# Second MLP product of nine token blocks as seven half-size products, with activation sums on VectorE

## The chip, the cores and the metric

The kernel runs on one core of a Trainium2 chip. The core has a matrix engine (PE, "TensorE"), three engines for elementwise work (DVE = "VectorE", ACT = "ScalarE", POOL = "GpSimd"), a queue engine that issues transfers (SP), and DMA engines that move data between HBM and on-chip memory. Matmul results go into PSUM, eight banks of 512 fp32 columns on 128 partitions; everything else lives in SBUF. The metric is device time of one execution in microseconds (us), lower is better.

## What is computed

Windowed attention with four sink tokens, then an MLP with the activation h·sigmoid(1.702h) and no biases. Cut to what matters:

```python
scores = q @ k.T / 8                        # 4 batches, 8 heads, 768 tokens, 64 wide
keep = (pos_k < 4) | (0 <= pos_q - pos_k < 128)
x = softmax(where(keep, scores, -1e9)) @ v  # -> 3072 tokens x 512
h = x @ w_in                                # 512 -> 2048
g = h / (1 + exp(-1.702 * h))
out = g @ w_out                             # 2048 -> 512
```

## The kernel before

The 3072 tokens are worked on in twelve blocks (`NK` = 12) of 256 tokens (`TB`), three to a batch. For a block `k` the work is: `load` (q, k, v from HBM, then casts to fp16, mostly on POOL from block 2 on), `turn` (q and k transposed: on PE for blocks 0 to 3, by a transposing DMA from block 4 on), `scores` (matmuls into PSUM, exp on ACT into the `at` tiles, the window mask on DVE), `back` (attention times v on PE, `reciprocal` and the normalising multiplication on DVE, transpose to `xT`, by DMA from block 3 on), `mm1` (first MLP product) and `mm2` (second).

`mm1(k)` has eight slices `s`. A slice is two groups of four matmuls with 256 columns into one PSUM bank (L736), a tanh on ACT (L748) and a scalar_tensor_tensor on DVE (L750) that writes one slice of `gT`, twice the activated value in fp16. `mm2(k)` takes the two halves of 128 tokens one after the other (`j`). Each is 16 accumulating matmuls with 512 columns (L765): the stationary operand is 128x128 of `gT`, the moving one a row slice of `w_out16`. ACT then copies the bank, times 0.5, to `osb` (L784), and SP issues two writes of 64 rows (L795). A block has thus 64 matmuls of 256 columns in L736 and 32 of 512 columns in L765.

The order of instructions on each engine is not the program's. Every piece of work is an `Op` with dependencies, a priority and a guessed duration. `Plan.run` plays these through a list scheduler, which also gives out the PSUM banks: seven when the constant masks hold one, with limits by class ("h" for `mm1`, "o" for `mm2`, "s" for scores and so on). The resulting order is then fixed; on the chip each engine runs its list in that order and waits on semaphores where it must. An operation with several possible engines (`plan.any`) gets the one that the plan finds best.

Buffers are rings, and an operation that overwrites a slot depends on the readers of what stood there (`reuse`, `uses`): `qk32`/`v32` (loaded data, RS = 3 slots), `at` (RA = 6), `gT` (RG = 5), `osb` (RO = 3 tiles of 128 tokens). The transfers of the start are chained by hand: a load or weight transfer waits for an earlier one to land (`gates`). The first weight transfer `w0` waits for one of the four q/k pieces of block 1, `o_first[-2]`.

Of the kernel before, what the change touches and what calls it, by code (L numbers as in the profile page):

```python
# [14 lines left out]
P = 128  # L15
# [45 lines left out]
class Plan:  # L61
# [4 lines left out]
    def op(self, eng, dur, lat, fn, deps=(), prio=0.0, acq=None, rel=(), kind=""):  # L66
        return self.any({eng: (dur, lat)}, lambda _: fn(), deps, prio, acq, rel, kind)
# [135 lines left out]
def kernel(  # L203
# [24 lines left out]
    PAIRED_FROM, RR = 2, 3  # L228
    KT, KX, AHEAD = globals().get('OPT',{}).get('KT',4), 3, globals().get('OPT',{}).get('AHEAD',0)
    RB, KM = 4, globals().get('OPT',{}).get('KM',2)  # L230
    RS, RQ, RV, RA, RX, RG, RTH, RO = 3, 2, 4, 6, 3, 5, 3, 3

    pool = ctx.enter_context(tc.tile_pool(name="sb", bufs=1))
    psp = ctx.enter_context(tc.tile_pool(name="ps", bufs=1, space=bass.MemoryType.PSUM))
# [3 lines left out]
    def ring(name, n, shape, dt):  # L238
        return [pool.tile(list(shape), dt, name=f"{name}{i}") for i in range(n)]
# [11 lines left out]
    vs16 = pool.tile([P, B, NP, 2, E], FP16, name="vs16")  # L251
    ks16 = pool.tile([P, B, NP, 32], FP16, name="ks16")
    vs32 = pool.tile([P, B, E], FP32, name="vs32")
    qk32 = ring("qk32", RS, (P, 2, H, 2, D), FP32)
    v32 = ring("v32", RS, (P, H, 2, D), FP32)
    qk16 = ring("qk16", RQ, (P, 2, 2, H, D), FP16)
    v16 = ring("v16", RV, (P, 2, H, E), FP16)
    at = ring("at", RA, (P, 2, 512), FP16)
# [4 lines left out]
    xT = ring("xT", RX, (P, NP, TB), FP16)  # L263
    th = ring("th", RTH, (P, 512), FP16)
    gT = ring("gT", RG, (P, NF, TB), FP16)
    osb = ring("osb", RO, (P, d_model), FP32)
    bank = [psp.tile([P, 512], FP32, name=f"bank{i}") for i in range(8)]

    plan = Plan(8, {"m": 1, "s": 5, "t": 4, "a": 2, "x": 2, "h": RTH, "o": 2})
    op = plan.op  # L270
    half = bank

    def f32(o, i=0):
        return bank[o.banks[i]]
# [372 lines left out]
    def back(k, p):  # L647

        b, r = divmod(k, R)
        u = NP * k + p  # L650
        base = attend(k, 2 * p)
        h8 = L / 8
        A, As = at[u % RA], ats[k % 3]
        vt, vp = v16[k % RV], v16[(k - 1) % RV]

        def avp():
            return f32(o_a)[:, 0 : 4 * E].rearrange("s (j h e) -> s j h e", j=2, h=2)

        def av():
            for j in range(2):  # L660
                if r:
                    blocks = [[(vp, 1, 0), (vt, 0, P)], [(vt, 0, 2 * P), (vt, 1, 3 * P)]][j]
                else:
                    blocks = [[(vt, 0, 0)], [(vt, 0, P), (vt, 1, 2 * P)]][j]
                for i in range(2):
                    mms = [(As[:, bass.ts(j, P)], vs16[:, b, p, i])] if r else []
                    mms += [(A[:, i, c : c + P], src[:, jj, 2 * p + i]) for src, jj, c in blocks]
                    for n, (a_, v_) in enumerate(mms):
                        nc.tensor.matmul(avp()[:, j, i], a_, v_, start=(n == 0), stop=(n == len(mms) - 1))  # L669
# [17 lines left out]
        o_r = op("DVE", 93, 190, lambda: nc.vector.reciprocal(out=rc, in_=avp()[:, :, :, D]),  # L687
                 [o_a], prio=base - 1.2 * h8, kind="rcp")
        o_n = op("DVE", 340, 430, lambda: nc.vector.tensor_tensor(  # L689
            out=X, in0=avp()[:, :, :, 0:D], in1=rc.to_broadcast((P, 2, 2, D)), op=ALU.mult),  # L690
            [o_r] + ([] if k < KX else o_xT["xb", k]), prio=base - 1.2 * h8, rel=[(o_a, 0)], kind="xn")
# [25 lines left out]


    o_g = {}
    n_o = [0]  # L720

    def mm1(k):
        X = xT[k % RX]
# [30 lines left out]
    def mm2(k):  # L754
        b, r = divmod(k, R)
        g = gT[k % RG]
        for j, c0, c1 in ((0, 0, 512), (1, 0, 512)) if k < NK - 1 else ((0, 0, 512), (1, 0, 384), (1, 384, 512)):
            w = c1 - c0
            last = w < d_model
            holder = []  # L760
            prev = None
            for s in range(NS):
                def f(s=s, j=j, holder=holder, c0=c0, c1=c1, w=w):
                    for Fi in (2 * s, 2 * s + 1):
                        nc.tensor.matmul(  # L765
                            f32(holder[0])[:, 0:w], g[:, Fi, bass.ts(j, P)], w_out16[:, Fi, c0:c1],
                            start=(Fi == 0), stop=(Fi == NF - 1),
                        )
                deps = [o_g[k, s], o_w[4 + s // 2]] + ([prev] if prev else [])
                o = op("PE", 2 * pe_ns(w), pe_ns(w) + w / 2.4 + 166, f, deps,  # L770
                       prio=nominal(k + 1, 4 * j + s / 2) + 3 + c0 / 100 * L, acq=None if s else ("o", 1), kind="mm2")
                uses("gT", k % RG, o)
                holder.append(o)
                prev = o
            if not c0:
                oi = n_o[0] % RO
                n_o[0] += 1
                war = reuse("osb", oi)
            O = osb[oi]
# [12 lines left out]
            for i in range(2):  # L792
                eng = "ACT" if i and k == NK - 1 and j else "SP"
                def f(O=O, i=i, row=row, c0=c0, c1=c1, dma=nc.scalar if eng == "ACT" else nc.sync):
                    dma.dma_start(  # L795
                        out[row : row + P, c0:c1].rearrange("(p i) f -> i p f", i=2)[i], O[64 * i : 64 * i + 64, c0:c1]
                    )
                o_d = op(eng, 590, (420, 4), f, o_c, prio=prio, kind="out")
                uses("osb", oi, o_d)

    for j_ in range(8):
        weights(j_, load_at(f"w{j_}"))
    for k_ in range(NK):
        load(k_)
        turn(k_)
        for ps_ in [(0,), (1,), (2,), (3,)] if k_ < PAIRED_FROM else [(0, 1), (2, 3)]:
            scores(k_, ps_)
        for p_ in range(NP):
            back(k_, p_)
        if k_ >= 1:  # L810
            mm1(k_ - 1)
        if k_ >= 2:
            mm2(k_ - 2)
    mm1(NK - 1)
    mm2(NK - 2)
# [82 lines left out]
```

The softmax here doesn't subtract the row's maximum and nothing guards it: scores larger than these inputs give would overflow.

## Time and profile before

Four runs: median 223.15 us, from 221.97 to 224.37.

| from the profile of one execution | |
|---|---|
| this execution's own time | 224.81 us |
| span of the profile | 223.0 us |
| granted TensorE clock, mean | 0.992 of full speed |
| matmuls of the first product (L736) | 768, 100.1 us busy |
| matmuls of the second product (L765, all forms) | 400, 99.8 us busy |
| tanh on ACT (L748) | 96, 603 ns each |
| ACT copies of the second product, 512 columns (L784) | 23, 604 ns each |
| normalising on DVE (L689, both targets) | 48, 422 ns each |
| idle time of ACT ahead of tanh, for PE | 62.5 us |
| DMA traffic | 36.54 MB |

How to read it. A line such as "L765 PE MATMUL bank<-w_out,gT 128\*128 128x512 f16 x368 | 96.3, 379" is a group of like instructions: source line, engine, operation, what it writes and reads, shape, count, then busy time in us and mean duration in ns. Matmuls overlap in the array, so the duration of one is longer than the distance from one to the next. On DVE and ACT too one instruction's record overlaps the next one's a little. Where this text needs what an engine can carry, it takes start-to-start distances out of the timeline. A timeline line is: start us, length us, engine, source line, operation, what it writes and reads, count; in brackets the idle time before and what ended it.

### The profile page before, as it was taken

How to read it: one execution, taken by the hardware profiler on the slowest of the kernel's cores; microseconds unless marked ns; L12 is line 12 of the kernel's file. 1: busy time of each engine (PE TensorE's matmuls, PEld its weight loads, DVE VectorE, ACT ScalarE, POOL GpSimd, SP SyncE). 2: the span in 40 equal slices, each digit the busy share in tenths (PEclk: the TensorE clock that was granted, in tenths of full speed). 3: DMA queues.
4: the chain of work that ended last, by engine and by line, in shares of the span. 5: the costliest groups of instructions: out<-in, count | busy, mean ns of one | idle time of the engine just before them, and what ended most of it. 6: DMA issues, size and time to landing. Idle time of an engine off the chain costs nothing.

```text
span 223.0 us, 5209 instructions
## 1 busy us (share of the span) xinstructions
PE 215.6 (97%) x2066; PEld 145.1 (65%) x2066; DVE 125.8 (56%) x274; ACT 125.6 (56%) x243; POOL 87.2 (39%) x150
## 2 busy tenths in 40 slices
PE   7977999999999999999999999999999999999993
PEld 2445887577766766766666766766667766766642
DVE  3665686278855755665555655765564665634310
ACT  2667655396746764655575575565476475544330
POOL 3568440846991773901923935706600000000000
PEclk9996999999999999999999999999999999999999
DMA  5999999989949869379579289299352222221223
GB/s 195 331 235 205 207 300 240 321 239 235 206 99 218 240 127 273 95 148 255 146 160 303 60 160 309 51 188 285 73 120 49 47 50 47 50 57 37 50 47 94
DMA packets 65911, 36.54 MB, mean 164 GB/s; under 512 B 27968, under 2 KB 61120, under 8 KB 65888
## 3 DMA queue, kind: packets, MB, share of 16 engines
q1 hardware_dynamic: 60848, 30.19, 54.6%
q0 software_dynamic: 4592, 5.37, 12.7%
q10 hardware_dynamic: 448, 0.66, 1.0%
q8 instruction: 16, 0.26, 0.4%
q14 instruction: 7, 0.06, 0.1%
HBM read 27.56 MB, written 6.29 MB: 152 GB/s over the span
## 4 chain that ended last, share of the span: by engine, by line
PE 89%; DMA 1%; ACT 0%; SPq 0%; DVE 0%; issue 0%
PE bank L736 38%; PE bank L765 36%; PE bank L669 7%; PE bank L604 5%; DMA out_dram<-osb 1%; PE bank L532 1%; PE bank L708 1%; PE bank L584 1%; PE bank L596 0%; ACT osb L784 0%; SPq L795 0%; PE bank L325 0%; DVE osb L786 0%
## 5 line engine op out<-in xcount | busy, mean ns | idle before, releaser
L736 PE MATMUL bank<-xT,w_in 128*128 128x256 f16 x768 | 100.1, 273 | 0.0
L765 PE MATMUL bank<-w_out,gT 128*128 128x512 f16 (+2 forms) x400 | 99.8, 371 | 0.0
L748 ACT ACTIVATE th<-bank 128x512 f16<-128x512 f32 x96 | 57.7, 603 | 63.1 <-PE bank L736 62.5
L750 DVE SCALAR_TENSOR_TENSOR gT<-th,bank 128x512 f16<-128x512 f16 x96 | 65.6, 683 | 48.8 <-ACT th L748 47.8
L736 PEld LDWEIGHTS <-w_in 128*128 128x128 f16 x768 | 73.2, 98 | 24.0 <-issue 1.7
L286 POOL CAST qk<-qk 64x512 f16<-64x512 f32 (+1 forms) x74 | 44.8, 609 | 45.3 <-DMA qk<-in_q_dram 42.2
L629 ACT ACTIVATE at<-bank 128x512 f16<-128x512 f32 (+1 forms) x96 | 48.8, 569 | 11.1 <-PE bank L604 10.8
L765 PEld LDWEIGHTS <-gT 128*128 128x128 f16 x400 | 36.1, 98 | 23.3 <-issue 1.4
L636 DVE TENSOR_TENSOR at<-at,bank 128x1024 f16<-128x1024 f16 (+1 forms) x40 | 25.7, 643 | 22.8 <-ACT at L629 22.8
L286 POOL CAST v<-v 64x512 f16<-64x512 f32 (+1 forms) x43 | 26.2, 610 | 10.9 <-DMA v<-in_v_dram 8.9
L669 PE MATMUL bank<-v,at 128*128 128x65 f16 x352 | 21.8, 196 | 2.2 <-ACT at L629 2.0
L669 PEld LDWEIGHTS <-at 128*128 128x128 f16 x352 | 18.1, 99 | 6.3 <-issue 2.1
L784 ACT ACTIVATE osb<-bank 128x512 f32<-128x512 f32 (+1 forms) x24 | 14.4, 600 | 11.0 <-PE bank L765 11.0
L689 DVE TENSOR_TENSOR xb<-bank,rcp 128x256 f16<-128x256 f32 x36 | 15.2, 422 | 0.7
L669 PE MATMUL bank<-vs,ats 128*128 128x65 f16 x128 | 15.3, 196 | 0.0
L604 PEld LDWEIGHTS <-blkT 64*128 64x128 f16 x256 | 8.1, 95 | 9.3 <-issue 7.8
L669 PEld LDWEIGHTS <-ats 128*128 128x128 f16 x128 | 12.3, 100 | 2.0
L604 PE MATMUL bank<-blkT 64*128 64x256 f16 x192 | 13.6, 246 | 0.0
L687 DVE RECIPROCAL rcp<-bank 128x4 f32<-128x4 f32 x48 | 8.4, 177 | 4.7 <-PE bank L669 3.6
L846 PE MATMUL bank<-zero 128*128 128x512 f16 x19 | 6.4, 503 | 1.2 <-DVE zero L304 1.2
L286 ACT COPY blkT<-bank 128x256 f16<-128x256 f16 (+1 forms) x12 | 5.0, 469 | 4.1 <-PE bank L532 4.1
L604 PE MATMUL bank<-blkT,blkT 64*128 64x128 f16 x64 | 7.3, 224 | 0.0
(43 smaller groups left out, 68.9 us busy)
## 6 DMA issues: line engine op xcount, KB each, us to landing
v<-in_v_dram SPq DMA_DIRECT2D x12, 512.0 KB, 7.1
out_dram<-osb SPq DMA_DIRECT2D x46, 128.0 KB, 2.4
qk<-in_q_dram SPq DMA_DIRECT2D x8, 512.0 KB, 5.2
qk<-in_k_dram SPq DMA_DIRECT2D x8, 512.0 KB, 6.4
w_in<-in_moe_w_in_dram POOLq DMA_DIRECT2D x4, 512.0 KB, 8.5
w_out<-in_moe_w_out_dram POOLq DMA_DIRECT2D x4, 512.0 KB, 11.8
qk<-in_q_dram SPq DMA_DIRECT2D x6, 256.0 KB, 5.0
qk<-in_k_dram SPq DMA_DIRECT2D x4, 256.0 KB, 5.2
```

Source lines behind the costliest of these rows:

```text
L286: {"POOL": nc.gpsimd.tensor_copy, "DVE": nc.vector.tensor_copy, "ACT": nc.scalar.copy}[e](out=out, in_=in_)
L604: nc.tensor.matmul(f32(o_s, 2 * n + i)[:, c : c + w], src[d, j], Q[d].rearrange("d j s -> d (j s)")[:, q0 : q0 + w], start=k >= KM, stop=T ...
L629: nc.scalar.activation(out=A[:, i, 0:W], in_=f32(o_s, 2 * n + i)[:, 0:W], func=AF.Exp, scale=scale)
L636: nc.vector.tensor_tensor(out=A[:, :, 0:W], in0=A[:, :, 0:W], in1=mask(c0, c0 + W).unsqueeze(1).to_broadcast((P, 2, W)), op=ALU.mult,)
L669: nc.tensor.matmul(avp()[:, j, i], a_, v_, start=(n == 0), stop=(n == len(mms) - 1))
L687: o_r = op("DVE", 93, 190, lambda: nc.vector.reciprocal(out=rc, in_=avp()[:, :, :, D]), [o_a], prio=base - 1.2 * h8, kind="rcp")
L689: o_n = op("DVE", 340, 430, lambda: nc.vector.tensor_tensor(out=X, in0=avp()[:, :, :, 0:D], in1=rc.to_broadcast((P, 2, 2, D)), op=ALU.mult ...
L736: nc.tensor.matmul(f32(holder[0])[:, bass.ts(e, TB)], w_in16[:, c, bass.ts(Fi, P)], X[:, c] if k < KX else X2[:, :, c], start=(c == 0), st ...
L748: o_t = op("ACT", 477, 600, lambda first=first: nc.scalar.activation(out=th[first.places[0]], in_=f32(first), func=AF.Tanh, scale=0.851), ...
L750: o_g[k, s] = op("DVE", 590, 700, lambda first=first, s=s: nc.vector.scalar_tensor_tensor(out=g[:, 2 * s : 2 * s + 2].rearrange("p a t -> ...
L765: nc.tensor.matmul(f32(holder[0])[:, 0:w], g[:, Fi, bass.ts(j, P)], w_out16[:, Fi, c0:c1], start=(Fi == 0), stop=(Fi == NF - 1),)
L784: nc.scalar.mul(O[:, c0:c1], f32(holder[0])[:, 0:w], 0.5)
```

## The change

Blocks 2 to 10 replace `mm2` by `mm2_by_seven`; blocks 0, 1 and 11 keep `mm2`. The product of a 256x2048 activation block with the 2048x512 weights is cut in two along tokens, along the contraction (even and odd slices of 128) and along the output columns. The 2x2 by 2x2 block product is then done with seven products in place of eight:

- Of the weights, four combinations are formed once (`forms_of_w`): t1 = b12-b11, t2 = b22-t1, t3 = b22-b12, t4 = b21-t2. That is 16 operations of 128x512. Three of the four live in what was the third load slot (tile `third`), which only block 2's load uses any more.
- Of each block's activations, four combinations are formed (`forms_of_g`): s1 = a21+a22, s2 = s1-a11, s3 = a11-a21 (written over a21 in `gT`), s4 = a12-s2; 16 tensor_tensor operations of 128x256 per block, planned on DVE.
- The products s1·t1, a11·b11, s4·b22, s2·t2, s3·t3, a12·b21, a22·t4 are eight matmuls of 256 columns each. Five go into one bank in three stages. After each stage ACT copies what the bank holds, times 0.5, into `part`, and PE then adds the next stage on top. The other two go into a second bank. DVE ends with two operations that scale a bank and add `part`, and SP issues four writes.

Cut to its core:

```diff
-    RS, RQ, RV, RA, RX, RG, RTH, RO = 3, 2, 4, 6, 3, 5, 3, 3
+    RS, RQ, RV, RA, RX, RG, RTH, RO = 3, 2, 4, 4, 3, globals().get('OPT',{}).get('RG',3), 3, 2
+    KS, LASTS = globals().get('OPT',{}).get('KS',2), globals().get('OPT',{}).get('LASTS',NK-1)
...
+    third = pool.tile([P, 3 * H * 2 * D], FP32, name="third")
+    qk32 = ring("qk32", RS - 1, (P, 2, H, 2, D), FP32)
...
+    gF = ring("gF", 2, (P, NS, 3, P), FP16)
+    part = pool.tile([P, 1024], FP32, name="part")
...
-    osb = ring("osb", RO, (P, d_model), FP32)
+    osb = ring("osb", RO, (P, 2 * d_model), FP32)
-    plan = Plan(8, {"m": 1, "s": 5, "t": 4, "a": 2, "x": 2, "h": RTH, "o": 2})
+    plan = Plan(8, {"m": 1, "s": 5, "t": 4, "a": 2, "x": 2, "h": RTH, "o": OPT_("NO", 3)})
...
-        sl = k % RS
+        sl = k if k < RS else (k - 1) % (RS - 1)
...
-        o_n = op("DVE", 340, 430, lambda: nc.vector.tensor_tensor(
-            out=X, in0=avp()[:, :, :, 0:D], in1=rc.to_broadcast((P, 2, 2, D)), op=ALU.mult),
+            for j in range(2):
+                for i in range(2):
+                    nc.scalar.activation(out=X[:, j, i], in_=avp()[:, j, i, 0:D], func=AF.Copy, scale=rc[:, j, i : i + 1])
+        o_n = plan.any({"DVE": (340, 430), **({"ACT": (430, 550)} if OPT_("XA", 3) <= k else {})}, normal,
...
+    def forms_of_g(k):
...
+            for o_, a, b_, what in ((s1, a21, a22, ALU.add), (s2, s1, a11, ALU.subtract), (a21, a11, a21, ALU.subtract), (s4, a12, s2, ALU.subtract)):
...
+    def mm2_by_seven(k):
...
+        m51 = run(2, lambda s: [(0, F[:, s, 0], wf[0][:, s]), (1, G[:, s, 0], W[:, s, 0, 0])], hr,
+                  lambda S: fg(0, S) + fw(0, S), True, ("o", 1))
+        o_1 = op("ACT", 477, 600, lambda: nc.scalar.mul(Z[:, N : 3 * N], f32(hr[0]), 0.5), [m51] + reuse("part", 0), prio=at(), kind="y")
+        m36 = run(2, lambda s: [(0, F[:, s, 2], W[:, s, 1, 1]), (1, F[:, s, 1], wf[1][:, s])], hr,
+                  lambda S: [o_1] + fg(3, S) + fg(1, S) + fw(1, S), False)
+        o_2 = op("ACT", 263, 390, lambda: nc.scalar.mul(Z[:, 0:N], f32(hr[0])[:, N : 2 * N], 0.5), [m36, o_1], prio=at(), kind="y")
+        m7 = run(4, lambda s: [(1, G[:, s, 1], wf[2][:, s])], hr, lambda S: [o_2] + fg(2, S) + fw(2, S), False)
+        o_3 = op("ACT", 263, 390, lambda: nc.scalar.mul(Z[:, 3 * N : 4 * N], f32(hr[0])[:, N : 2 * N], 0.5), [m7, o_2], prio=at(), kind="y")
+        o_v = op("DVE", 600, 700, lambda: nc.vector.scalar_tensor_tensor(
+            out=O.rearrange("p (n c) -> p n c", n=4)[:, 1::2], in0=f32(hr[0]).rearrange("p (n c) -> p n c", n=2), scalar=0.5,
...
+        m24 = run(2, lambda s: [(0, G[:, s, 2], W[:, s, 1, 0]), (1, G[:, s, 3], wf[3][:, s])], hq, lambda S: fw(3, S), True, ("o", 1))
+        o_u = op("DVE", 600, 700, lambda: nc.vector.scalar_tensor_tensor(
...
-            g = o_first[OPT.get("WG", -2)]
+            g = o_first[OPT.get("WG", -1)]
```

More of the change, by code (lines that the diff above doesn't have):

```diff
@@ L253 @@
     vs32 = pool.tile([P, B, E], FP32, name="vs32")
-    qk32 = ring("qk32", RS, (P, 2, H, 2, D), FP32)
-    v32 = ring("v32", RS, (P, H, 2, D), FP32)
+    third = pool.tile([P, 3 * H * 2 * D], FP32, name="third")
+    qk32 = ring("qk32", RS - 1, (P, 2, H, 2, D), FP32)
+    v32 = ring("v32", RS - 1, (P, H, 2, D), FP32)
+    qk32.append(third[:, 0 : 2 * H * 2 * D].rearrange("p (e h i d) -> p e h i d", e=2, h=H, i=2))
+    v32.append(third[:, 2 * H * 2 * D :].rearrange("p (h i d) -> p h i d", h=H, i=2))
+    wf = [third[:, 1024 * n : 1024 * n + 1024].bitcast(FP16).rearrange("p (s c) -> p s c", s=NS) for n in range(3)]
+    wf += ring("wf", 1, (P, NS, d_model // 2), FP16)
+    gF = ring("gF", 2, (P, NS, 3, P), FP16)
+    part = pool.tile([P, 1024], FP32, name="part")
     qk16 = ring("qk16", RQ, (P, 2, 2, H, D), FP16)
@@ L265 @@
     gT = ring("gT", RG, (P, NF, TB), FP16)
-    osb = ring("osb", RO, (P, d_model), FP32)
+    osb = ring("osb", RO, (P, 2 * d_model), FP32)
     bank = [psp.tile([P, 512], FP32, name=f"bank{i}") for i in range(8)]
-    plan = Plan(8, {"m": 1, "s": 5, "t": 4, "a": 2, "x": 2, "h": RTH, "o": 2})
+    OPT_ = globals().get("OPT", {}).get
+    plan = Plan(8, {"m": 1, "s": 5, "t": 4, "a": 2, "x": 2, "h": RTH, "o": OPT_("NO", 3)})
     op = plan.op
@@ L688, in back, with normal @@
                  [o_a], prio=base - 1.2 * h8, kind="rcp")
-        o_n = op("DVE", 340, 430, lambda: nc.vector.tensor_tensor(
-            out=X, in0=avp()[:, :, :, 0:D], in1=rc.to_broadcast((P, 2, 2, D)), op=ALU.mult),
+        def normal(eng):
+            if eng == "DVE":
+                nc.vector.tensor_tensor(out=X, in0=avp()[:, :, :, 0:D], in1=rc.to_broadcast((P, 2, 2, D)), op=ALU.mult)
+                return
+            for j in range(2):
+                for i in range(2):
+                    nc.scalar.activation(out=X[:, j, i], in_=avp()[:, j, i, 0:D], func=AF.Copy, scale=rc[:, j, i : i + 1])
+        o_n = plan.any({"DVE": (340, 430), **({"ACT": (430, 550)} if OPT_("XA", 3) <= k else {})}, normal,
             [o_r] + ([] if k < KX else o_xT["xb", k]), prio=base - 1.2 * h8, rel=[(o_a, 0)], kind="xn")
@@ L719 @@
     o_g = {}
-    n_o = [0]
     def mm1(k):
@@ L775, in mm2 @@
             if not c0:
[L776 to L779, printed above, removed]
+                war = reuse("osb", (k % RO, j))
+            O = osb[k % RO][:, bass.ts(j, d_model)]
             row = k * TB + j * P
@@ L798, in mm2, with forms_of_w, f @@
                 o_d = op(eng, 590, (420, 4), f, o_c, prio=prio, kind="out")
-                uses("osb", oi, o_d)
+                uses("osb", (k % RO, j), o_d)
+    def forms_of_w():
+        W = w_out16.rearrange("p (s e) (h c) -> p s e h c", e=2, h=2)
+        free = [o for (kk, _, _), o in o_cqk.items() if kk == 2] + [o for p in range(NP) for o in o_cv[2, p]]
+        for j in range(4):
+            x = slice(2 * j, 2 * j + 2)
+            b11, b12, b21, b22 = (W[:, x, e, h] for e in range(2) for h in range(2))
+            t1, t2, t3, t4 = (wf[n][:, x] for n in range(4))
+            for n, (o_, a, b_, what) in enumerate(((t1, b12, b11, ALU.subtract), (t2, b22, t1, ALU.subtract),
+                                                   (t3, b22, b12, ALU.subtract), (t4, b21, t2, ALU.subtract))):
+                def f(eng, o_=o_, a=a, b_=b_, what=what):
+                    (nc.gpsimd if eng == "POOL" else nc.vector).tensor_tensor(out=o_, in0=a, in1=b_, op=what)
+                deps = [o_w[4 + j]] + ([o_wf[j, n - 1]] if n in (1, 3) else [])
+                if n == 3:
+                    deps.append(o_wf[j, 1])
+                o_wf[j, n] = plan.any({"POOL": (1110, 1250), "DVE": (450, 550)}, f, deps + (free if n < 3 else []),
+                                      prio=nominal(KS + 1, OPT_("WFP", -9) + j), kind="wf")
@@ new lines, in forms_of_g, with f @@
+    def forms_of_g(k):
+        g, F = gT[k % RG], gF[k % 2]
+        G = g.rearrange("p (s e) (t q) -> p s (e t) q", e=2, t=2)
+        war = reuse("gF", k % 2)
+        w = OPT_("GW", 2)
+        for s in range(0, NS, w):
+            x = slice(s, s + w)
+            a11, a21, a12, a22 = (G[:, x, n] for n in range(4))
+            s1, s2, s4 = (F[:, x, n] for n in range(3))
+            last = [o_g[k, i] for i in range(s, s + w)] + war
+            four = []
+            for o_, a, b_, what in ((s1, a21, a22, ALU.add), (s2, s1, a11, ALU.subtract), (a21, a11, a21, ALU.subtract), (s4, a12, s2, ALU.subtract)):
+                def f(eng, o_=o_, a=a, b_=b_, what=what):
+                    (nc.gpsimd if eng == "POOL" else nc.vector).tensor_tensor(out=o_, in0=a, in1=b_, op=what)
+                o = plan.any({e: {"POOL": (280 * w, 280 * w + 120), "DVE": (OPT_("GD", 105) * w + 60, OPT_("GD", 105) * w + 170)}[e] for e in OPT_("GE", "DVE").split()},
+                             f, last, prio=nominal(k, s + OPT_("GF", 5)) + 3, kind="gf")
+                last = [o]
+                four.append(o)
+            for i in range(s, s + w):
+                o_f[k, i] = four
@@ new lines, in mm2_by_seven, with run, f, at @@
+    def mm2_by_seven(k):
+        g, F, O, Z = gT[k % RG], gF[k % 2], osb[k % RO], part
+        G = g.rearrange("p (s e) (t q) -> p s (e t) q", e=2, t=2)
+        W = w_out16.rearrange("p (s e) (h c) -> p s e h c", e=2, h=2)
+        N = d_model // 2
+        u = [0]
+        def run(n_s, what, first, deps, fresh, acq=None):
+            prev = None
+            holder = first
+            for s0 in range(0, NS, n_s):
+                def f(s0=s0):
+                    for s in range(s0, s0 + n_s):
+                        for half, lhs, rhs in what(s):
+                            nc.tensor.matmul(f32(holder[0])[:, bass.ts(half, N)], lhs, rhs, start=fresh and s == 0 and half == what(0)[0][0],
+                                             stop=s == NS - 1, skip_group_check=True)
+                n = n_s * len(what(0))
+                o = op("PE", n * pe_ns(N), (n - 1) * pe_ns(N) + N / 2.4 + 166, f,
+                       deps(range(s0, s0 + n_s)) + ([prev] if prev else []), prio=at(),
+                       acq=None if holder else acq, kind="mm2")
+                u[0] += 1
+                if not holder:
+                    holder.append(o)
+                uses("gT", k % RG, o)
+                uses("gF", k % 2, o)
+                prev = o
+            return prev
+        def at():
+            return nominal(k + 1, 8 * u[0] / 14) + 3
+        def fw(n, S):
+            return [o_wf[s // 2, n] for s in S]
+        def fg(n, S):
+            return [o_f[k, s][n] for s in S]
+        hr, hq = [], []
+        war = reuse("osb", (k % RO, 0)) + reuse("osb", (k % RO, 1))
+        m51 = run(2, lambda s: [(0, F[:, s, 0], wf[0][:, s]), (1, G[:, s, 0], W[:, s, 0, 0])], hr,
[8 more added lines that the diff above has]
+            out=O.rearrange("p (n c) -> p n c", n=4)[:, 1::2], in0=f32(hr[0]).rearrange("p (n c) -> p n c", n=2), scalar=0.5,
+            in1=Z[:, 0 : 2 * N].rearrange("p (n c) -> p n c", n=2), op0=ALU.mult, op1=ALU.add),
+            [m7, o_3] + war, prio=at(), rel=[(hr[0], 0)], kind="oc")
+        m24 = run(2, lambda s: [(0, G[:, s, 2], W[:, s, 1, 0]), (1, G[:, s, 3], wf[3][:, s])], hq, lambda S: fw(3, S), True, ("o", 1))
+        o_u = op("DVE", 600, 700, lambda: nc.vector.scalar_tensor_tensor(
+            out=O.rearrange("p (n c) -> p n c", n=4)[:, 0::2], in0=f32(hq[0]).rearrange("p (n c) -> p n c", n=2), scalar=0.5,
+            in1=Z[:, 2 * N : 4 * N].rearrange("p (n c) -> p n c", n=2), op0=ALU.mult, op1=ALU.add),
+            [m24, o_3] + war, prio=at(), rel=[(hq[0], 0)], kind="oc")
+        uses("part", 0, o_v)
+        uses("part", 0, o_u)
+        for j in range(2):
+            row = k * TB + j * P
+            for i in range(2):
+                def f(i=i, j=j, row=row):
+                    nc.sync.dma_start(
+                        out[row : row + P].rearrange("(p i) f -> i p f", i=2)[i], O[64 * i : 64 * i + 64, bass.ts(j, d_model)])
+                o_d = op("SP", 590, (420, 4), f, [o_v, o_u], prio=nominal(k + 1, 8) + 4, kind="out")
+                uses("osb", (k % RO, j), o_d)
@@ L801, with second @@
+    o_wf, o_f = {}, {}
+    def second(k):
+        if KS <= k < LASTS:
+            mm2_by_seven(k)
+        else:
+            mm2(k)
     for j_ in range(8):
@@ L811 @@
             mm1(k_ - 1)
+            if KS <= k_ - 1 < LASTS:
+                forms_of_g(k_ - 1)
+        if k_ == 2:
+            forms_of_w()
         if k_ >= 2:
-            mm2(k_ - 2)
+            second(k_ - 2)
     mm1(NK - 1)
-    mm2(NK - 2)
-    mm2(NK - 1)
+    if LASTS == NK:
+        forms_of_g(NK - 1)
+    second(NK - 2)
+    second(NK - 1)
     loads += o_vl + [o_more]
```

## Prediction

> **What bounds the kernel now.** I read the shares by engine first, then the chain of waits that ended last, then the costliest groups, then the timeline of the engines that the change loads.
>
> ```profile
> PE 215.6 (97%) x2066; PEld 145.1 (65%) x2066; DVE 125.8 (56%) x274; ACT 125.6 (56%) x243; POOL 87.2 (39%) x150
> ...
> PE 89%; DMA 1%; ACT 0%; SPq 0%; DVE 0%; issue 0%
> ```
>
> PE is busy all the time and is also the chain: nothing but matmuls sets the end, once the start (some 18 us) is over. So a matmul saved is time saved, unless another engine becomes late. The price of a matmul is its distance to the next, which the PE timeline gives:
>
> ```profile
> 105.41 1.03 PE L765 MATMUL bank<-w_out,gT 128*128 128x512 f16 x4
> 106.27 0.34 PE L669 MATMUL bank<-v,at 128*128 128x65 f16 x6
> 106.45 1.04 PE L736 MATMUL bank<-xT,w_in 128*128 128x256 f16 x8
> 107.33 1.03 PE L765 MATMUL bank<-w_out,gT 128*128 128x512 f16 x4
> ```
>
> Eight of 256 columns take 107.33 - 106.45 = 0.88 us, four of 512 take 105.41 to 106.27 = 0.86 us: about 109 and 215.5 ns each. For the DVE:
>
> ```profile
> 59.42 0.55 DVE L636 TENSOR_TENSOR at<-at,bank 128x768 f16<-128x768 f16 x1
> 59.88 0.18 DVE L687 RECIPROCAL rcp<-bank 128x4 f32<-128x4 f32 x1
> 59.97 0.66 DVE L750 SCALAR_TENSOR_TENSOR gT<-th,bank 128x512 f16<-128x512 f16 x1
> 60.55 0.42 DVE L689 TENSOR_TENSOR xb<-bank,rcp 128x256 f16<-128x256 f32 x1
> 60.88 0.68 DVE L750 SCALAR_TENSOR_TENSOR gT<-th,bank 128x512 f16<-128x512 f16 x1
> ```
>
> Back to back, an instruction costs its record less some 0.09 us: mask (768) 0.46, reciprocal 0.09, scalar_tensor_tensor 0.58, normalising 0.33. And the POOL, which casts in trains:
>
> ```profile
> 135.91 5.17 POOL L286 CAST qk<-qk 64x512 f16<-64x512 f32 x8 [2.36 <-DMA qk<-in_q_dram]
> 141.15 2.59 POOL L286 CAST v<-v 64x512 f16<-64x512 f32 x4
> ```
>
> Twelve casts of 0.65 us a block, 7.8 us without a gap, then idle.
>
> [...] The DVE work of blocks before reads at most one large operand from SBUF (the other is a PSUM bank, the constant masks too), so the trace does not show this form. [...]
>
> ```profile
> 16.18 0.43 DVE L286 CAST v<-v 64x512 f16<-64x512 f32 x1 [1.40 <-DMA v<-in_v_dram]
> 16.28 0.79 POOL L286 CAST v<-v 64x512 f16<-64x512 f32 x1 [1.85 <-DMA v<-in_v_dram]
> ```
>
> A POOL cast that began 0.10 us into a DVE cast took 0.79 us where the others take 0.61. [...] No activation with a pointer is in the trace.
>
> **The change part by part.**
>
> *PE.* Removed: 32 x 215.5 = 6.90 us a block. Added: 7 products x 8 matmuls of 256 = 56 x 109 = 6.10 us. Nine blocks: 9 x 0.79 = **-7.1 us**, all on the path. Three scores batches (L604, same kind) in the before trace stand at 56.40, 104.16 and 151.87 us, three blocks apart: 15.9 us a block, so 15.1 after.
>
> *Sums of the activations, on DVE.* All 16 per block stand on DVE in the changed order. Masks of 1024 and 768 columns take 684 and 545 ns, 0.543 ns a column, so 256 columns make 267 ns, or 0.18 us back to back; s2 reads s1, so that pair costs 0.30. A group of four: 0.30 + 3 x 0.18 = 0.84, a block 3.4 us. DVE's other work in a block: scalar_tensor_tensor 8 x 0.58, masks 4 x 0.59, reciprocals 4 x 0.09, normalising 4 x 0.33 = 8.7 us. The two closing operations are the L750 kind, 2 x 0.58 = 1.2. Normalising moved to ACT: the changed order has 11 of 36 there, -1.2 x 0.33 = -0.4. Sum 12.9 us of 15.1: it fits, with 2.2 us to spare, before the lock. The lock: casts cover 7.8 of 15.1 us, 52%. 16 x 0.52 = 8.3 sums a block meet one. Bounds: nothing if they always find the gaps; a whole cast each, 8.3 x 0.61 = 5.1 us. I take half a cast, 2.5 us, since other DVE work stands between most sums and the phase is then random. That is 0.3 over what is free, in the 6.5 blocks or so before POOL's last cast at 160 us: +2 us at most if none of it is absorbed; I take **+1.3**. Where DVE is late, L750 is late next, then the bank it frees, then L736.
>
> *Sums of the weights.* 16 of 128x512: 13 on DVE at 545 - 139 = 406 ns, 0.32 back to back = 4.1 us, 3 on POOL (nearest: its two-input 128x520 row, about 1.06 us each). They run between about 42 and 60 us, with block 2's sums. DVE is busy 4.9 us in 40 to 50 and 8.2 in 50 to 60; with 4.1 + 3.4 that is 20.6 of 20, and 4.8 in 60 to 70 leaves room to catch up. Between 0 and 2 us; I take **+0.4**.
>
> *ACT.* Per block 2 x 0.604 of copies become one of 512 and two of 256 columns (0.60 + 2 x 0.39): nothing to speak of, ACT has over 40% idle. But each stage of PE now waits for such a copy, and everything behind it on PE waits too. From the changed order and the prices above, 1.2 to 1.7 us of other matmuls stand between stage one and two, against 0.27 (PE to ACT in the timeline) + 0.60 + some 0.1 = 0.97: covered. Between stage two and three 0.8 to 1.2 us, against 0.27 + 0.39 + 0.1 = 0.76: barely. A tanh in front of the copy shows. A moved normalising is four activations of 64 columns; [...] mostly covered by ACT's idle time, so **+0.4**. Normalising frees DVE and delays the transpose of `xT` by at most 0.6 us.
>
> *Nothing for these.* Load slots 3 to 2: a load now waits for the casts of two blocks back; the casts that began at 87.32 ended at 95.27 and the load with that slot would be issued at 114.21. `at` 6 to 4, `gT` 5 to 3: the changed order has the readers of the old content several us ahead of the writers, on PE itself for `at`, a whole block for `gT`. SP: the four writes of a block now follow both closing operations at once, and the two transposing DMAs and the loads behind them wait; SP waited for ACT's copies there already (one run of writes from 134.26 lasts 9.44 us). If DVE is late by more than a few us, the cover is gone and PE waits for `xT`. The end (block 11) is the old product. The weights' gate moves one 256 KB piece, about 0.7 us by the casts of those pieces at 8.84 and 9.57: PE stands 2.05 us at 15.9 for block 1's v, which would land sooner, weights later; -0.5 to +0.5, taken as 0.
>
> Sum: -7.1 + 1.3 + 0.4 + 0.4 = -5.0. The profiled execution took 224.8 us (span 223.0): it would become 219.8. It lay 1.7 above the median of 223.15, which becomes **218.1 us**.
>
> **The rivals.**
>
> *DVE becomes the bound (slower).* [...] With 0.61 for half of those that meet casts and 0.3 for the rest, 8.3 x 0.46 = 3.8 us a block. Over the 2.2 spare by 1.6 in 6.5 blocks: +10.4, time 223.15 - 7.1 + 10.4 = **226.5**. It cancels the gain from 0.21 us mean wait per sum (3.3 us a block). For it: the 52%, and the chains s1, s2. Against: in the changed order other work often stands between, and after 160 us POOL is silent.
>
> *The waits are hidden (the full gain).* The lock costs under 2.2 us a block and ACT keeps up: **216.0**. For it: DVE's and ACT's idle time, and no PE stall now after the start.
>
> *PE stalls at every stage wait.* 0.3 us at nine third stages plus eleven late normalisings of 0.2 us more than taken: about +4.5, **222**. For it: the margin of under 0.1 us.
>
> *It does not do what it says*: the counts in the order are as stated, 504 matmuls of 256 columns for 288 of 512, so this is out.
>
> **How the numbers follow.** Forecast as summed, or up to 220: 0.45. Full gain: 0.22. Stage stalls: 0.16. DVE the bound: 0.17, reaching from 222.5 to 234 (a whole cast each: +18.9). A measurement of this kernel can tell about 1%, 2.2 us. Faster than 220.9: 0.45 + 0.22 and half of the stalls = 0.75. Slower than 225.4: most of the DVE case, 0.13. Between: 0.12. The range, 215.4 (full gain and a better start) to 223.3, leaves out most of the DVE case and little below.
>
> **What the profile will show.** PE busy down by about 7 us; matmuls of 256 columns in the second product at 109 ns. The sums: mean near 267 ns means no lock, near 420 (267 + 2.5/16) the forecast, over 480 the rival; longer in the casts' trains than after 160 us. Casts longer than 0.61 us. DVE near 14 to 15 us of each 15. PE idle for `mul` of `part`, or L736 waiting for L750, where stalls are. The forecast is wrong if blocks 3 to 8 take over 15.9 us each.

## The result, and the profile after

Over all comparisons the changed kernel took 222.93 us (median of 41 runs, 221.25 to 226.18) and the kernel before 222.19 us (66 runs). The ratio is 1.0024, with a 95% interval of 1.0008 to 1.0039: no gain, if anything a loss of up to 0.4%. Forecast were 218.1 us and a range of 215.4 to 223.3; the time lies inside the range, but in the case "about the same", which had 0.12. The ratio leaves out slow executions; both profiles are of such ones (225.51 us after, 224.81 before), each with one stretch of 3.4 us at half clock before 23 us, which cancels between them.

From the page of the kernel after: the busy shares, then the shares of the chain that ended last, then the costliest form of the activation sums.

```profile
PE 210.6 (94%) x2282; PEld 165.6 (74%) x2282; DVE 178.9 (80%) x437; ACT 135.9 (61%) x298; POOL 92.7 (41%) x152
...
PE 60%; DVE 23%; DMA 6%; ACT 4%; issue 3%; SPq 2%; DVEq 0%; ACTq 0%
...
L846 DVE TENSOR_TENSOR gF<-gF,gT 128x256 f16<-128x256 f16 x36 | 13.6, 377 | 0.8
```

The span of this execution is 223.4 us, against 223.0 before. PE's busy time fell by 5 us, but it now leaves 6% of the span idle instead of 3%. The chain, 89% matmuls and no DVE before, now runs through DVE for 23%.

How much of the matmul saving arrived can be counted. I summed over all matmuls the distance that each needs to the next when nothing holds it up, its pitch. It is measured in both traces together, on the matmuls with a stationary operand of 128x128, as the mean of the distances within 3 ns of their median: 29.3 ns for 65 columns, 55.8 for 128, 109.1 for 256, 162.5 for 384, 215.8 for 512. The sum is 216.08 us before and 208.92 after, that is **-7.2 us**, against -7.1 forecast. I then summed what the actual distances between starts exceed it by: 2.11 us before, 9.67 after, that is **+7.6 us**. (This excess can be negative in a stretch: the eight matmuls on 64 rows at 107.39 us take 0.44 us together, 0.66 by these pitches.) The gain was made and given back. Up to 30 us both kernels lose the same, 6.9. The difference arises at 50 to 60 us (1.9 us), 60 to 90 us (3.0) and 90 to 170 us (2.8); after that there is none.

The waits of PE between 74 and 170 us, with total, times and longest. The kernel before has no entry there but "issue" (no releaser that the profile shows); the kernel after has, beside that:

```profile
PEld L678 <- DVE at L645: 1.9, 3, 0.8
...
PE bank L678 <- DVE at L645: 0.9, 2, 0.5
PE bank L593 <- DVE osb L903: 0.8, 2, 0.5
...
PE bank L751 <- DVE gT L765: 0.2, 1, 0.2
```

Apart from 0.2 us all of it is DVE: the mask (L645), the closing operation (L903), the scalar_tensor_tensor of `mm1` (L765). None of it is an ACT copy of `part`. DVE by stage, in windows of 10 us (columns as in the first line):

```profile
core 0: us, PE busy (x) PEld busy (x) DVE busy (x) ACT busy (x) POOL busy (x), PEclk, DMA share, GB/s
50.00:60.00 10.00, 8.33 (x103) 5.65 (x101) 10.00 (x25) 6.51 (x15) 8.94 (x14) 1.00 0.81 221
60.00:70.00 10.00, 9.54 (x81) 6.55 (x79) 10.00 (x23) 4.79 (x11) 9.31 (x15) 1.00 0.41 80
...
110.00:120.00 10.00, 9.23 (x97) 7.80 (x95) 8.86 (x20) 6.43 (x17) 7.03 (x12) 1.00 0.73 188
...
170.00:180.00 10.00, 10.00 (x126) 8.78 (x124) 9.23 (x28) 5.90 (x12) 0.00 (x0) 1.00 0.20 49
```

From 50 to 70 us DVE is busy without a gap and PE is not. From 50 to 170 us DVE is busy for 112.2 of 120 us (73.2 before), far more than its 80% over the whole span says. At 110 us DVE has a gap now and then, and PE still loses 0.8 us. At 170 us POOL is silent; DVE does more instructions (28 against 20) in about the same busy time, and PE is full.

Two places in the timeline show how. First the weight sums (L825). While POOL does two of them, two of DVE's take 1.12 and 1.37 us instead of 0.41; the mask queued behind is late, and PE waits for it:

```profile
52.83 2.44 POOL L825 TENSOR_TENSOR third<-w_out 128x512 f16<-128x512 f16 x2
...
53.15 1.12 DVE L825 TENSOR_TENSOR third<-w_out,third 128x512 f16<-128x512 f16 x1
...
54.19 1.37 DVE L825 TENSOR_TENSOR third<-w_out 128x512 f16<-128x512 f16 x1
...
55.68 0.54 DVE L645 TENSOR_TENSOR at<-at,bank 128x768 f16<-128x768 f16 x1
...
56.27 0.36 PE L678 MATMUL bank<-v,at 128*128 128x65 f16 x6 [1.67 <-DVE at L645]
```

Second the activation sums (L846) at the end of a train of casts that lasts to 72.3 us. Those that meet a cast take 0.69 to 0.73 us, those after it 0.28:

```profile
69.51 2.83 POOL L295 CAST v<-v 64x512 f16<-64x512 f32 x4
...
71.14 0.69 DVE L846 TENSOR_TENSOR gF<-gT,gF 128x256 f16<-128x256 f16 x1
...
71.75 0.73 DVE L846 TENSOR_TENSOR gT<-gT 128x256 f16<-128x256 f16 x1
72.41 0.28 DVE L846 TENSOR_TENSOR gF<-gT 128x256 f16<-128x256 f16 x1
72.61 0.28 DVE L846 TENSOR_TENSOR gF<-gT,gF 128x256 f16<-128x256 f16 x1
...
72.75 0.28 PE L870 MATMUL bank<-third,gF 128*128 128x256 f16 x1 [0.95 <-DVE gF L846]
```

That a DVE sum of two SBUF operands waits for a POOL instruction beside it, the prediction's "lock", was an assumption beforehand; the trace of the kernel before has no such sum. The trace of the kernel after shows the wait: all 25 activation sums over 0.5 us end 0.139 to 0.150 us after the end of a POOL instruction, and all seven weight sums over 0.5 us 0.274 to 0.282 us after one. DVE operations with a PSUM bank as one operand show no such wait: L765 takes 649 to 690 ns both beside POOL's work (44 of them) and without it (52). POOL pays too: its 64x512 casts of q and k rose from 609 to 633 ns on average.

### The profile page after: what moved, and what is told of

Its sections match the earlier page's. It is cut to its first block, busy times and chain, and to the rows that moved or that the text cites. A ratio compares the mean times of both kernels' runs of the same rounds, so it can differ in the third digit from the quotient of the medians.

```text
span 223.4 us, 5881 instructions
## 1 busy us (share of the span) xinstructions
PE 210.6 (94%) x2282; PEld 165.6 (74%) x2282; DVE 178.9 (80%) x437; ACT 135.9 (61%) x298; POOL 92.7 (41%) x152
## 4 chain that ended last, share of the span: by engine, by line
PE 60%; DVE 23%; DMA 6%; ACT 4%; issue 3%; SPq 2%; DVEq 0%; ACTq 0%
PE bank L751 27%; PE bank L870 18%; DVE gT L765 6%; DMA v<-in_v_dram 6%; PE bank L780 5%; DVE gF L846 5%; PE bank L678 5%; PE bank L613 3%; DVE third L825 2%; DVE at L645 2%; ACT th L763 2%; DVE gT L846 2%; SPq L416 2%; DVE osb L903 1%; ACT at L638 1%
## 5 line engine op out<-in xcount | busy, mean ns | idle before, releaser
L765 DVE SCALAR_TENSOR_TENSOR gT<-th,bank 128x512 f16<-128x512 f16 x96 | 65.2, 680 | 17.4 <-ACT th L763 16.6
L870 PE MATMUL bank<-third,gF 128*128 128x256 f16 x144 | 34.4, 273 | 1.4 <-DVE gF L846 1.4
L870 PE MATMUL bank<-w_out,gT 128*128 128x256 f16 x144 | 34.3, 273 | 0.0
L870 PEld LDWEIGHTS <-gT 128*128 128x128 f16 x288 | 27.7, 98 | 4.1 <-issue 0.9
L645 DVE TENSOR_TENSOR at<-at,bank 128x1024 f16<-128x1024 f16 (+1 forms) x40 | 25.2, 636 | 4.9 <-ACT at L638 4.9
L295 POOL CAST v<-v 64x512 f16<-64x512 f32 (+1 forms) x38 | 23.9, 628 | 3.1 <-DMA v<-in_v_dram 1.3
L870 PEld LDWEIGHTS <-gF 128*128 128x128 f16 x216 | 20.7, 98 | 4.7 <-DVE gF L846 1.9
L780 PE MATMUL bank<-w_out,gT 128*128 128x512 f16 (+2 forms) x112 | 23.6, 349 | 0.0
L678 PEld LDWEIGHTS <-at 128*128 128x128 f16 x352 | 17.2, 98 | 6.1 <-DVE at L645 4.8
L870 PE MATMUL bank<-wf,gT 128*128 128x256 f16 x72 | 17.2, 273 | 0.0
L870 PE MATMUL bank<-w_out,gF 128*128 128x256 f16 x72 | 17.1, 273 | 0.0
L780 PEld LDWEIGHTS <-gT 128*128 128x128 f16 x112 | 9.8, 98 | 7.0 <-issue 0.3
L846 DVE TENSOR_TENSOR gF<-gF,gT 128x256 f16<-128x256 f16 x36 | 13.6, 377 | 0.8
```

Of the source, the lines that this page charges most:

```text
L295: {"POOL": nc.gpsimd.tensor_copy, "DVE": nc.vector.tensor_copy, "ACT": nc.scalar.copy}[e](out=out, in_=in_)
L645: nc.vector.tensor_tensor(out=A[:, :, 0:W], in0=A[:, :, 0:W], in1=mask(c0, c0 + W).unsqueeze(1).to_broadcast((P, 2, W)), op=ALU.mult,)
L765: o_g[k, s] = op("DVE", 590, 700, lambda first=first, s=s: nc.vector.scalar_tensor_tensor(out=g[:, 2 * s : 2 * s + 2].rearrange("p a t -> ...
L780: nc.tensor.matmul(f32(holder[0])[:, 0:w], g[:, Fi, bass.ts(j, P)], w_out16[:, Fi, c0:c1], start=(Fi == 0), stop=(Fi == NF - 1),)
L846: (nc.gpsimd if eng == "POOL" else nc.vector).tensor_tensor(out=o_, in0=a, in1=b_, op=what)
L870: nc.tensor.matmul(f32(holder[0])[:, bass.ts(half, N)], lhs, rhs, start=fresh and s == 0 and half == what(0)[0][0], stop=s == NS - 1, skip ...
```

## The experiments

The theory: DVE's two-input sums wait for POOL, and what stands behind them on DVE comes too late for PE. The rivals: the ACT copies between the stages; the smaller rings and the moved gate; the sheer number of DVE instructions without any wait for POOL. Each time is a median, each ratio is to the kernel before, run on the same chip, with its 95% interval. Times come from different chips, so a gain in us is a difference of ratios times 222.2 where nothing else is said. The first experiments cut one suspect to two columns each, so that instruction, order and semaphores stay and only the length goes; these kernels leave work out and don't compute the result.

**POOL's casts short** (blocks 4 and later; their attention then works on old data):

```diff
-copy(eng, C[...].rearrange("s p (h d) -> s p h d", h=2), dst[...].rearrange("s (p h) d -> s p h d", h=2))
+copy(eng, C[...].rearrange("s p (h d) -> s p h d", h=2)[:, :, :, 0:2], dst[...].rearrange("s (p h) d -> s p h d", h=2)[:, :, :, 0:2])
...
-copy(eng, w16[64 * i : 64 * i + 64, j, h, 0:D], dv[64 * j : 64 * j + 64, h, i])
+copy(eng, w16[64 * i : 64 * i + 64, j, h, 0 : D if k < KT else 2], dv[64 * j : 64 * j + 64, h, i, 0 : D if k < KT else 2])
```

> The changed kernel with POOL's casts cut to two columns per head from block 4 on (its v casts too), so attention of those blocks works on old data. Order, waits and DVE's instructions stay; POOL reads SBUF hardly at all after some 52 us. If the lock [...] makes DVE late (lock theory), the sums' mean falls from 360 to about 285 ns, PE's lost time after 50 us falls from 7 us to 2 or less, and the time to 217 to 218.5. If DVE simply has too much work of its own (load theory), the sums get shorter but PE still waits: 221 or more.

Measured: 217.64 us, ratio 0.9802 (0.9745 to 0.9859). The activation sums by operand form, with shortest, median and longest duration in ns, in the kernel after:

```profile
L846 DVE TENSOR_TENSOR gF<-gT x36: 276/291/694, 65.2 to 201.2; 128x256 f16<-128x256 f16 x36
L846 DVE TENSOR_TENSOR gF<-gF,gT x36: 256/292/735, 65.6 to 201.6; 128x256 f16<-128x256 f16 x36
L846 DVE TENSOR_TENSOR gT<-gT x36: 277/284/731, 67.1 to 201.8; 128x256 f16<-128x256 f16 x36
L846 DVE TENSOR_TENSOR gF<-gT,gF x36: 260/284/1149, 68.0 to 202.0; 128x256 f16<-128x256 f16 x36
```

and with short casts:

```profile
L846 DVE TENSOR_TENSOR gF<-gT x36: 277/285/578, 62.0 to 193.4; 128x256 f16<-128x256 f16 x36
L846 DVE TENSOR_TENSOR gF<-gF,gT x36: 258/291/295, 62.3 to 193.7; 128x256 f16<-128x256 f16 x36
L846 DVE TENSOR_TENSOR gT<-gT x36: 258/284/297, 63.5 to 193.9; 128x256 f16<-128x256 f16 x36
L846 DVE TENSOR_TENSOR gF<-gT,gF x36: 255/283/286, 64.3 to 194.1; 128x256 f16<-128x256 f16 x36
```

The medians are the same; the long tail is gone but for two sums (578 and 379 ns), and with it 2.2% of the time (from 1.0024 to 0.9802, 4.9 us). DVE executes as many instructions as in the kernel after, so their number alone is not the cause. What PE still lost after 30 us is in the main one pause of 2.05 us at 52 us, at the weight sums.

**Weight sums short** (the products then read plain weights):

```diff
-(nc.gpsimd if eng == "POOL" else nc.vector).tensor_tensor(out=o_, in0=a, in1=b_, op=what)
+(nc.gpsimd if eng == "POOL" else nc.vector).tensor_tensor(out=o_[:, :, 0:2], in0=a[:, :, 0:2], in1=b_[:, :, 0:2], op=what)
```

> The changed kernel with the 16 sums of the weights cut to two columns each, at their places in the order, and the products reading plain weights in their stead. If the sums of the weights, in one burst of 50 to 63 us together with block 2's own sums, are what makes DVE late at first (burst theory), the stalls between 50 and 90 us (4.9 us) go and those after 100 us stay: about 218 to 219. If the sums of every block are what costs, the burst is only a small part: 221 to 222.

Measured: 219.76 us, 0.9893 (0.9832 to 0.9954): 1.3%, 2.9 us, from sixteen instructions. PE has no excess left at 50 to 60 us.

**Activation sums short** (the same edit at L846; the products then read `gT`):

> The changed kernel with the 16 sums per block cut to two columns per slice, at their places in the order, and the products reading gT in their stead. If DVE's lateness is all that eats the gain (lock or load theory), PE keeps nearly all of the 7.1 us: 216 to 217.5, with a stall left at 50 to 65 us from the sums of the weights. If PE's waits for ACT's three copies per block, or the late normalising on ACT, cost the time, it stays at 220 or more.

Measured: 219.14 us, 0.9868 (0.9807 to 0.9929), less of a gain than expected. The ACT copies and all stages are still there, and no wait of PE for them shows. In the profiled execution the rest went into the pause at the weight sums and something behind it. The windows of this kernel around the pause:

```profile
52.00:54.00 2.00, 0.28 (x8) 0.05 (x2) 2.00 (x4) 2.00 (x6) 1.94 (x3) 1.00 1.09 308
54.00:56.00 2.00, 1.83 (x22) 1.44 (x23) 2.00 (x7) 0.75 (x2) 1.88 (x3) 0.79 1.15 294
56.00:58.00 2.00, 2.00 (x11) 1.42 (x10) 1.42 (x5) 0.47 (x2) 1.82 (x4) 0.50 0.64 196
58.00:60.00 2.00, 2.00 (x16) 1.51 (x14) 1.68 (x3) 0.89 (x2) 1.84 (x4) 0.86 0.00 0
```

The column behind POOL is the granted clock. After PE stood still for 2.05 us it ran below full clock. What is missing from full clock in the last three windows is 2 x (0.21 + 0.50 + 0.14) = 1.7 us, or 3.4 us at half clock: the pause cost 3.75 us in all. But this execution was the longest of four (219.91 us, granted clock 0.992); the other three had 0.997 to 1.0, so the half clock is not what holds the median. Why the median lies 3.2 us above the kernel with casts and weight sums short (below, by the ratios), and not only the 2 us of the pause, stays open.

**The old product, with the new buffers and gate** (`KS`, the first block with seven products, and `XA`, the first with normalising on ACT, both 99, so none; no weight sums):

> The changed kernel with the old second product in all blocks, no sums of weights, and all normalising on DVE: what is left of the change is the shorter rings (load slots, at, gT), osb in larger tiles, a third bank for the second product and the later gate of the first weights. If these cost nothing: 222 to 223, as before. If the rings or the gate cost time (buffer theory): 225 or more, and then the product itself gained that much more.

Measured: 222.35 us, 1.0008 (0.9984 to 1.0033). Rings, gate and the larger output tiles cost nothing within some 0.3%; this rival is out. (The four late writes of a block are not in this kernel; they are in the next.)

**Casts and weight sums short together:**

> Both cuts together: POOL's casts from block 4 on at two columns per head, and the sums of the weights at two columns with the products reading plain weights (so the result is not the reference's in either respect). If lock and burst are all there is, PE's lost time after 30 us is that of the old product and the whole of the 7.1 us shows: 215 to 216. If a third cause (waits for ACT's copies) is left, 217 or more.

Measured: 215.64 us (two runs), 0.9724 (0.9684 to 0.9765). Against the old product with the same buffers that is 222.35 - 215.64 = 6.7 us by the times and 0.0284 x 222.2 = 6.3 by the ratios, nearly the whole 7.2. All DVE sums of the activations, all ACT copies, stages and writes are in this kernel, so no third cause of size is left. The two parts alone gave 4.9 and 2.9 us, 7.8 in all; together they give 0.0300 x 222.2 = 6.7. They may overlap by about 1 us, since the weight sums in one burst delay the blocks behind it; the intervals are too wide to show it.

**Fewer, longer activation sums** (`GW` = 4 in place of 2: 72 of 128x512):

> The changed kernel with each sum over four slices (128x512) in place of two (128x256): 8 sums a block, 72 in all. Same elements, half the instructions, so at most half as many waits for a POOL cast and half the fixed cost on DVE: recorded time of the sums from 52 to some 34 us. Lock theory and load theory both: 219 to 221. If the sums come too late for the products because each now waits for four slices: 222 or more, with PE waiting for gF.

Measured: 222.21 us, 1.0021 (0.999 to 1.0051), no better, against 219 to 221 expected. The sums take 418 to 424 ns at the median (284 to 292 for half the columns) and 792 to 829 at the longest, so per column they are cheaper, and PE's excess after 60 us fell by 2 us. But in this order the pause at 52 us was 2.04 us, in the profiled execution with half clock behind it, some 3.7 us together. As 17 of the 20 executions had a granted clock of 0.997 or more, the half clock is not why the median is no better; that stays open.

**Only from block 8 on** (`KS` = 8, three blocks):

> The changed kernel with the seven products in blocks 8 to 10 only, where POOL is about to have no casts left (its last ends near 165 us). PE's saving is 3 x 0.79 = 2.4 us. Lock theory: nearly all of it shows, 220 to 220.5, since few sums meet a cast. Load theory: DVE is late here as well, 221.5 to 222.5.

Measured: 220.66 us, 0.9968 (0.9924 to 1.0011). By the ratio that is 0.7 us of the 2.4 that three blocks of matmuls are worth (0.9 against the old product with new buffers), and the interval reaches from no change to 1.7: the run doesn't decide between the two expectations. The weight sums run as early as before (44 to 62 us), but with block 2's activation sums gone and with lower priority PE's longest pause there is 0.27 us.

**Casts of v on ACT** (blocks 4 and later), to take a third of POOL's casts away:

> The changed kernel with the casts of v from block 4 on moved from POOL to ACT: POOL's trains shrink from twelve casts to eight, ACT gets four of 0.62 us a block. Lock theory: a third of the waits goes, PE's stalls after 60 us fall by a third or more: 220 to 221.5. If ACT becomes late by it (tanh later, then the bank of the first product): 222.5 or more.

Measured: 224.15 us, 1.0116 (1.0044 to 1.0188), slower, as was expected if ACT becomes late. Two casts now stand ahead of a tanh and of the exps on ACT, and PE waits for those:

```profile
82.51 1.25 ACT L295 CAST v<-v 64x512 f16<-64x512 f32 x2
83.79 0.60 ACT L763 ACTIVATE th<-bank 128x512 f16<-128x512 f32 x1
84.28 2.06 ACT L638 ACTIVATE at<-bank 128x512 f16<-128x512 f32 x4
...
85.42 0.29 PE L593 MATMUL bank<-blkT,ks 128*32 128x256 f16 x4 [1.80 <-ACT at L638]
```

ACT is 69% busy in this kernel, and still two casts in a row at the wrong place cost 2 us. The pause at the weight sums was there as well, 2.06 us, in the profiled execution with half clock behind it. The run says nothing against the waits for POOL; it put a new one beside them.

**Weight sums later, and on DVE alone** (priority -5 in place of -9, no POOL):

> The changed kernel with the sums of the weights on DVE alone and planned half a block later (behind other DVE work of the same time). Three sums of 1.15 to 1.25 us leave POOL, so DVE no longer waits over a whole one of them (two DVE sums of 1.1 and 1.4 us in the changed kernel), but DVE has 1 us more of its own. Burst theory with POOL's own sums as the worst part: stalls of 50 to 70 us fall from 2.7 to under 1, time 221 to 222. If only the amount of work in that stretch counts: no better, 222.5 to 223.5.

Measured: 222.78 us, 1.0011 (0.9958 to 1.0064). The pause at 52 us is gone (0.5 us of excess left at 50 to 60), but the sums now run into the next train of casts, beside block 2's activation sums:

```profile
59.69 5.06 POOL L295 CAST qk<-qk 64x512 f16<-64x512 f32 x7
...
62.79 0.69 DVE L846 TENSOR_TENSOR gF<-gF,gT 128x256 f16<-128x256 f16 x1
63.41 0.87 DVE L825 TENSOR_TENSOR third<-w_out,third 128x512 f16<-128x512 f16 x1
...
67.28 0.28 PE L870 MATMUL bank<-w_out,gT 128*128 128x256 f16 x1 [1.48 <-DVE gT L765]
```

Here the sums of both kinds wait for casts, and L765 is late instead of the mask. The run changes both the engine and the time of the weight sums, so by itself it doesn't separate them. For the pause all traces together point to one thing: in the five kernels where POOL does two long weight sums in a row between 50 and 55 us (the kernel after, and those with short casts, short activation sums, sums of four slices, and v on ACT) PE pauses there for 1.83 to 2.06 us. In the five others that do the sixteen sums in full, this one among them, no pause between 44 and 63 us is over 0.38. Without the pause the time was no better: in this run's trace PE's excess at 60 to 90 us is 2.7 us, against 1.7 in the kernel after.

**From block 4, 5 and 7 on**, with sums of four slices (`GW` = 4); from block 4 with the weight sums on DVE alone as well:

> Seven products in blocks 4 to 10, sums over four slices, weight sums on DVE alone: the burst and the first sums of activations are two blocks apart. PE saves 7 x 0.79 = 5.5 us. If the burst hurts only where it meets block 2's sums, PE's stalls at 50 to 65 us are gone and what is lost is the lock in blocks 4 to 7: 218.5 to 220. If the burst stalls PE by itself: 220.5 or more.

> As the changed kernel, but seven products in blocks 5 to 10 and sums over four slices. PE saves 6 x 0.79 = 4.7 us; lock in blocks 5 to 7 takes some 1 to 1.5: 218.5 to 219.5. If the lock takes all that a block gains while POOL casts, no better than from block 8: 220.5.

> Seven products in blocks 7 to 10, sums over four slices. PE saves 4 x 0.79 = 3.2 us, one block of them under POOL's casts: 219 to 220, if a block that is free of casts keeps all it gains. Worse than from block 5 if the lock leaves blocks 5 and 6 with a gain of their own, better if they lose by it.

| seven products in blocks | us | ratio to before (95%) |
|---|---|---|
| 4 to 10 | 220.76 | 0.9906 (0.9882 to 0.993) |
| 5 to 10 | 220.01 | 0.9888 (0.9789 to 0.9987) |
| 7 to 10 | 220.00 | 0.9874 (0.9835 to 0.9912) |

The first lies above the 218.5 to 220 that was expected, near the 220.5 that was to mean that the burst alone stalls PE. Its trace says otherwise: no pause over 0.4 us at 50 to 65, but one of 1.2 at 112 and one of 0.9 at 160, both for DVE's closing operation L903.

Fewer blocks are as good or better. From block 5 against the sums of four slices from block 2, 2.4 us of matmul saving are given up and 0.0133 x 222.2 = 3.0 us won (with an uncertainty of over 2 us): most of what was lost must lie in blocks 2 to 4 and the weight sums beside them. Two more blocks under POOL's casts (5 and 6) show no gain; the version from block 4 on is 0.8 us slower than that from block 5, but its weight sums stand elsewhere too, and the intervals overlap. The version from block 7 on is 1.3% faster than the kernel before. On its page DVE is 65% busy and the chain reads:

```profile
PE 91%; DVE 3%; ACT 3%; issue 1%; DVEq 0%
```

Four blocks are worth 4 x 0.79 = 3.2 us by the pitch of matmuls; 1.26% of 222.2 is 2.8.

## Why the prediction was wrong

*PE.* Right: -7.1 us forecast, -7.2 by the count of matmuls and their measured distance, and 6.3 to 6.7 us of time where the waits were taken away.

*Sums of the activations.* That the sums wait for POOL was right; the **conversion of waiting into time** (the term +1.3: wait less spare time, in the 6.5 blocks) **was wrong**, and it is the step that failed. The mean of a sum is 360 ns (377, 372, 349 and 342 in the four forms); 285 of it is the sum itself (267 forecast). So the wait is 75 ns a sum or 10.8 us in all, less than forecast: over 6.5 blocks 1.7 us a block instead of 2.5. It is very uneven: 25 of the 144 sums took over 500 ns, and they hold 9.8 of the 10.8 us. The mean is 390 ns before 160 us and 291 after. Back to back and not held up, sums start 0.20 to 0.21 us apart, and s2 0.31 to 0.33 behind s1 (0.18 and 0.30 forecast). By my own balance (2.2 us spare in a block) that should have cost nothing. It cost some 4 to 5 us (4.9 with the weight sums present, and 0.0169 x 222.2 = 3.8 between the kernel with short weight sums and the one with both short). I had set a mean wait against a mean spare time, 0.3 us of excess times 6.5 blocks. But DVE is 93% busy from 50 to 170 us, and full for stretches of 10 us and more. Waits come in trains with the casts, several sums one after the other, and a mask, L765 or L903 behind them is late at once, while the spare time comes later, when PE has already stood. I had named L750, now L765, as late next; the mask and the closing operation were late as well.

*Sums of the weights.* Forecast +0.4, with 2 as the upper bound; measured 2.9 us with what follows from it (1.7 where the casts are short: 0.0078 x 222.2). The prices of the single sums on DVE were right where nothing interfered (406 ns; shortest forms 389 to 416). I counted DVE's 20 us of work and looked no further: beside two of POOL's own sums in a row (1152 and 1332 ns), two of DVE's took 1116 and 1369 ns, directly ahead of a mask that PE waits for. DVE's order, which was known beforehand, has two weight sums directly ahead of that mask. Together the two terms and the +0.4 for ACT were put at 2.1 us and are 7.6 in the traces (the old product's kernel against the kernel after, from 30 us on). The difference of 5.5 us is the whole error: -5.0 forecast, +0.5 measured (0.0024 x 222.2).

*ACT.* The copies between the stages cost nothing: no wait of PE for them shows in the kernel after, and +0.4 and the rival of the stage stalls (222 us) fall. That this rival's time was close, and that the range took the measured time in, is luck: neither foresaw what happened. The price of a moved normalising was not shown by the trace of before, which has no such activation; in the trace of after the four take 322 ns each on average, start 0.20 to 0.21 us apart and hold ACT for some 0.93 us.

*What I costed at nothing* did cost nothing: the kernel with the old product and the new rings, gate and slots is at 1.0008. The start loses 6.9 us in both profiles, before and after.

*The rival "DVE becomes the bound"* (226.5) reckoned with the same waits for POOL's casts and put the loss right in kind: its loss of 10.4 us is nearer to the 7.6 than my 1.7. But it too needed waits above the spare time, with sums over 480 ns. For half of the sums that meet a cast it took a wait of 0.61 us; in the seven pairs of activation sums directly behind each other that were both over 0.5 us, the second was 0.35 to 0.45 us longer than its form's median without POOL's casts. The measured 360 (390 under the casts) lay below what I had named for the forecast (420), and yet the gain was gone: the mean of the sums was not the quantity that decides. (Small slips beside it: with a whole cast each the case reaches to 235, not 234, and the stage stalls come to 222.6. And the POOL cast of 0.79 us was 0.18 us longer than the others, where the whole rest of DVE's cast was 0.33; so that one pair does not show that POOL waits until DVE is through. Nothing hangs on these.) The other criterion did hold: the scores batches that stood at 104.16 and 151.87 us stand at 107.39 and 156.40 in the changed kernel, three blocks in 49.0 us, 16.3 a block, over the 15.9 that I had given as the sign of a wrong forecast.

## What to carry to other kernels

When matmul time is bought with work on another engine, it isn't enough that this work fits on average. Look in the changed order at who stands directly behind the new instructions, and set the longest run of waits that can come together against the lead that PE has at that point; here, with DVE 93% busy from 50 to 170 us, the lead didn't suffice. It can pay to make the change only where the other engine has room: here, with sums of four slices, it gained nothing from block 2 on and 0.9 to 1.3% when begun at block 4, 5 or 7 (begun at block 8, with sums of two slices, the gain isn't shown). DVE's sums of two SBUF operands took 291 ns on average once POOL's casts were nearly over, and 390 before; but the versions from block 4 and 5 gained under the casts too, so this is not the whole of it.

## What the runs showed of the hardware that I had not expected

- A DVE sum of 128x512 that is 406 ns alone took up to 1.37 us beside a POOL sum of 1.15 to 1.33 us. A 128x256 sum beside POOL's casts took up to 0.73 us in place of 0.28. The longest one, 1.15 us, stood beside another two-input sum of POOL, of 1.13 us, that had begun 0.13 us earlier and that the kernel before has too:

```profile
135.06 1.13 POOL L488 TENSOR_TENSOR vs<-vs,more 128x520 f16<-128x520 f32 x1
135.19 1.15 DVE L846 TENSOR_TENSOR gF<-gT,gF 128x256 f16<-128x256 f16 x1
```

- A pause of PE of 2.04 to 2.06 us was followed by half clock in three traces (about 3.4 us of it, 1.7 us lost), and in a fourth with the same pause, that of the short casts, by full clock. The profile of the kernel before has a pause of 2.2 us at 15.7 us, and 1.7 us lost behind it. The pause of 1.83 us in the kernel after had none behind it; but this kernel's profile has a half-clock stretch from 17.7 us, after two pauses of only 0.8 and 1.4 us between 12.9 and 15.6. So the length of one pause doesn't decide; what does, the traces don't show. In the profile of the short activation sums a stall of 2.05 us cost 3.75 with the half clock behind it.
